# Two layers of attention and routed feed-forward on one core: the first tile of the output projection is placed and ordered anew, and the steps between projection, routing and the next layer are spread differently

## The chip, the cores and the metric

The kernel runs on one core of one Trainium2 chip. The metric is the device time of that core in microseconds. The kernel before took 4644.64 us (median of three runs, 4642.4 to 4648.78). Engines are named as in the profile: PE is TensorE (PEld its weight loads), DVE VectorE, ACT ScalarE, POOL GpSimd, SP SyncE. SP, ACT and POOL also issue DMAs, each from a queue of its own that works in order; a "q" behind the name (SPq, ACTq) marks the engine's sequencer.

## What is computed

Two layers, each of softmax attention and of a feed-forward block for the 8 tokens with the highest router score; both layers use the same weights.

```python
def _A_ref(x, wqkv, wo):          # x: 1 x 2048 x 1024, 32 heads of 32
    q, k, v = ...                 # from x @ wqkv
    p = softmax(q k^T * Dh ** -0.5)
    return (p v) @ wo
def _B_ref(x, w_r, w_gate, w_up, w_down):
    r = x @ w_r                   # router score of each token
    idx = argsort(-r)[:8]
    y = (silu(x_sel @ w_gate) * (x_sel @ w_up)) @ w_down     # F = 3584
    y = y * sigmoid(r_sel)
    return x + scatter_add(0, idx, y)
for _ in range(2):
    x = x + _A_ref(layernorm(x), wqkv, wo)
    x = x + _B_ref(layernorm(x), w_r, w_gate, w_up, w_down)
```

## The kernel before

**Order of work.** The program order is written out by hand: each engine runs its instructions in the order in which the Python code issues them, and waits only on data and on buffers. A buffer of a pool is handed on when all users of its last tile are done. Every product in high precision is made of three: a float32 matrix is split into a rounded high part and the rest, the low part, and high x high, low x high and high x low are summed in PSUM. ACT makes the high part with a cast, DVE or POOL the low part with a subtraction.

**A layer** (`layer`, called with n = 0 and n = 1) has three stages.

1. *Projection of q, k, v.* 96 steps `k`, each 24 products of 128x512 (a pass). Four blocks `c` of 512 tokens; in the first block of the second layer, steps 8, 12, 16 and 20 also take the statistics of a further tile and normalise it (`ln_stat`, `ln_norm`, L707 to 712), and every even step splits the next weight block (`split_w`, L686: one ACT cast, one POOL subtraction of 128x2048) and loads another (`load_w`). `ln_stats` (L138) ends in two small POOL operations that give `rs`, for which `ln_norm` on DVE waits. `proj` (L764) ends with an ACT cast `hi` and a DVE subtraction `lo`.
2. *Attention.* 32 units (head group x query chunk) of 16 key tiles; for each tile scores, exponential into `P` (nine buffers), products with v, and a running sum `ACC` of the exponentials over the key tiles. For the last unit DVE alone adds tiles 1 to 13 to tile 0, and `sum_mm` (L972) lets PE sum over the keys: first the tiles in `DIRECT` (14, 15), then `ACC`. Sums go to DRAM, come back by halves (`sum_load`, a tile of 64x512), are inverted on DVE (`recip`, L1001) and go out again.
3. *Output projection*, 16 token tiles `t` (L1141 to 1202). Of a tile: `load_o` (output `ord` and inverted sums, from DRAM: one and four DMAs, two buffers), `scale_o` (DVE), `split_o` (ACT cast `ohl`, DVE subtraction), 48 products of 128x512 against the weights' high parts `woh` and low parts `wol`, in three runs over the eight weight rows (L1148), then on DVE the residual sum (L1168), statistics (L1177), `xn` (L1188) and the router score (L1192), which overwrites the PSUM tile. PSUM has two such tiles (`ps_pre`), so tile t+2 starts after tile t's L1192. `load_o(t + 4)` is issued on ACT. Before tile 0, ACT casts eight weight rows (L1122) and DVE and POOL make their low parts (L1129). The second half of the sums (`second`) lies in the place of `xn`, so that `xn` of tile 0 waits until it is written out.

**Where things lie.** Pools are stacked. In the first layer the pool `wf` (`ord`, `ohl`, `woh`) stands behind the next layer's projection pool, since that layer's generator `nxt` is started first (L1067 to 1074); `ord` of tile 0 then falls into `KS[1]`, the keys, which the last scores read. In the second layer `ord` is the first of `wf` and falls into `KS[1]` too. The three query buffers `q0`, `q1`, `q2` are used in turn by the units.

**What the layers share.** Layer 1 is a generator that runs a piece at each `next(nxt)` inside the last tiles of layer 0's output projection: load weights and four tiles, statistics and normalisation of tiles 0 to 3, split of the first weights, transposes (`ln_tr`, L714: PE, ACT high part, DVE low part L739). The feed-forward block of layer 0 is worked off inside layer 1's projection: `stage` is the routing, in pieces that end at `yield`; `first_stage` runs beside the tiles after `CT` = 9, `second_stage` in steps 3 to 9 of layer 1's projection, one piece a step. `stage` ends with a gather and a scatter of rows on POOL's queue (L314, L315), and the scatter waits for the gather's data. `second_stage` ends with L346 to L350 on DVE and PE. Then `tick` works off four feed-forward steps and `refill` loads their weights (at steps 10, 14, ... and 11, 15, ...), and `permutation` (L352, at steps 13 and 17) has POOL write three tiles of 8x8 (`vb`) for PE.

## Time and profile before

| what | value |
|---|---|
| median of three runs | 4644.64 us |
| the profiled execution | 4644.15 us |
| its span, first to last instruction | 4642.1 us |
| busy share: PE, DVE, ACT, POOL | 97%, 69%, 52%, 69% |
| mean granted PE clock | 0.988 |
| first projection, attention, output projection of layer 0 | about 0 to 570, 570 to 2036, 2036 to 2235 us |
| the same of layer 1 | about 2235 to 2885, 2885 to 4347, 4347 to 4537 us |
| last feed-forward block | about 4537 to 4642 us |

The profile is of one execution. A row of the timeline has the start in us from the span's start, the duration, the engine, the line of the code, the operation, what is written and read, the count of instructions that are merged in the row, and in brackets the engine's idle time before it with what ended that. A row of the waits has the waiting instruction, what it waited for, the sum of the waits in us, their number and the longest. A row of the windows has the busy time of each engine in a stretch with its instruction count, then the granted PE clock, the busy share of the DMA engines and GB/s.

### The profile page before, as it was taken

To read this page: it belongs to the slowest core of one execution; us is meant where nothing else is said; L and a number is where in the kernel's file an instruction comes from. 1 tells how busy PE (TensorE), PEld (TensorE's weight loads), DVE (VectorE), ACT (ScalarE), POOL (GpSimd) and SP (SyncE) were. 2 spreads that over 40 slices of the span, in tenths; PEclk is the share of its full clock that TensorE was granted. 3 is DMA by queue.
4 is the path that set the end of the run, shared out by engine and by line. 5 is a ranking of instruction groups with operands and counts; after the bars stand their busy time and mean duration, and the time that the engine had idled before them with its cause. 6 is when DMAs were issued, how large, how long until landed. Compare 5 with 4: busy or idle time off the path is not lost. (4 is left out here: it accounts for less than half of the span.)

```text
span 4642.1 us, 73520 instructions
## 1 busy us (share of the span) xinstructions
PE 4520.6 (97%) x29224; PEld 2688.0 (58%) x29224; DVE 3183.7 (69%) x4945; ACT 2428.9 (52%) x2568; POOL 3219.2 (69%) x1247
## 2 busy tenths in 40 slices
PE   9999999999999999989899999999999999999896
PEld 7888755555555555448667786555555555554572
DVE  2211588888888888876422215888888888887763
ACT  3322267676767667750122222776676767677400
POOL 4444288988989898844433342988888899898441
PEclk9999999999999999999899999999999999999997
DMA  6757477776877777658489774777777768676597
GB/s 202 207 175 209 131 162 168 156 174 143 179 153 158 171 153 169 158 139 230 133 289 291 236 216 129 164 158 165 160 161 160 171 147 180 150 169 159 150 250 310
DMA packets 329301, 833.50 MB, mean 180 GB/s; under 512 B 44118, under 2 KB 159830, under 8 KB 279790
## 3 DMA queue, kind: packets, MB, share of 16 engines
q1 hardware_dynamic: 275214, 476.95, 35.0%
q0 software_dynamic: 45216, 325.57, 34.6%
q10 hardware_dynamic: 8528, 26.29, 2.2%
q8 instruction: 229, 3.75, 0.3%
q14 instruction: 114, 0.93, 0.1%
HBM read 384.24 MB, written 119.37 MB: 108 GB/s over the span
## 5 line engine op out<-in xcount | busy, mean ns | idle before, releaser
L639 DVE TENSOR_REDUCE nm<-st 128x1 f32<-128x512 f32 x3916 | 2433.7, 683 | 374.0 <-PE st L631 368.2
L1031 ACT ACTIVATE P<-pre 128x1024 f32<-128x1024 f32 x2048 | 1986.2, 1022 | 720.8 <-PE pre L646 522.2
L967 POOL TENSOR_TENSOR acc<-acc,P 128x2048 f32<-128x2048 f32 x434 | 2103.8, 4848 | 80.4 <-DMA P<-P 72.5
L646 PE MATMUL pre<-q,ks 64*128 64x512 f32 (+1 forms) x8192 | 1142.7, 396 | 4.3 <-ACT P L1031 4.3
L957 PE MATMUL pv<-P,v 128*32 128x512 f32 x8192 | 1091.9, 605 | 5.1 <-DMA v<-vd 5.1
L631 PEld LDWEIGHTS st<-ks,q 64*128 64x128 f32 x3916 | 546.5, 184 | 906.6 <-DVE nm L639 764.7
L631 PE MATMUL st<-ks,q 64*128 64x512 f32 x3916 | 980.6, 469 | 0.4
L646 PEld LDWEIGHTS pre<-q,ks 64*128 64x128 f32 (+1 forms) x8192 | 770.8, 186 | 190.7 <-ACT P L1031 57.4
L970 POOL DMA_DIRECT2D P<-P x310 | 296.4, 956 | 264.1 <-PE st L631 193.0
L775 DVE TENSOR_TENSOR lo<-st,hi 128x512 fp32r<-128x512 f32 x128 | 88.5, 691 | 568.4 <-ACT hi L774 562.7
L697 POOL TENSOR_TENSOR ohl<-wraw,ord 128x2048 fp32r<-128x2048 f32 x48 | 220.6, 4597 | 338.0 <-ACT ord L694 329.4
L697 POOL TENSOR_TENSOR wl<-wraw,wh 128x2048 fp32r<-128x2048 f32 (+1 forms) x49 | 221.1, 4512 | 303.8 <-ACT wh L694 285.0
L774 ACT CAST hi<-st 128x512 fp32r<-128x512 f32 x128 | 75.4, 589 | 564.1 <-PE st L760 564.1
L957 PEld LDWEIGHTS pv<-P,v 128*32 128x32 f32 x8192 | 161.8, 108 | 261.6 <-issue 253.3
L967 POOL TENSOR_TENSOR acc<-P 128x2048 f32<-128x2048 f32 x62 | 294.7, 4753 | 9.1 <-ACT P L1031 9.1
L1157 PE MATMUL pre<-woh,ohl 128*128 128x512 f32 x1024 | 245.3, 398 | 25.9 <-DVE pre L1192 14.4
L1157 PEld LDWEIGHTS pre<-woh,ohl 128*128 128x128 f32 x1024 | 195.9, 192 | 72.5 <-issue 17.2
L760 PE MATMUL st<-xh,wh 128*128 128x512 f32 x512 | 201.2, 393 | 0.0
L760 PE MATMUL st<-xh,wl 128*128 128x512 f32 x512 | 199.5, 390 | 0.0
L760 PE MATMUL st<-xl,wh 128*128 128x512 f32 x512 | 199.3, 389 | 0.0
L1101 ACT CAST ohl<-ord 128x1024 fp32r<-128x1024 f32 x32 | 33.6, 1051 | 309.6 <-DVE ord L1093 184.7
L760 PE MATMUL st<-woh,ord 128*128 128x512 f32 x512 | 166.8, 401 | 0.0
(344 smaller groups left out, 3866.7 us busy)
## 6 DMA issues: line engine op xcount, KB each, us to landing
P<-P POOLq DMA_DIRECT2D x310, 1024.0 KB, 8.8
wraw<-in_A_wqkv_dram SPq DMA_DIRECT2D x96, 1024.0 KB
q<-qh SPq DMA_DIRECT2D x256, 128.0 KB
ks<-kh SPq DMA_DIRECT2D x112, 256.0 KB
vd<-vn SPq DMA_DIRECT2D x32, 512.0 KB
qh<-hi SPq DMA_DIRECT2D x64, 256.0 KB
ql<-lo SPq DMA_DIRECT2D x64, 256.0 KB
kh<-hi SPq DMA_DIRECT2D x64, 256.0 KB
```

The costliest lines, as they stand in the source:

```text
L631: pe.matmul(ps[b], Q[u][rows, i, 0, qt * 128:(qt + 1) * 128], KS[(u // QC) % 2][rows, i, 0, j * 512:(j + 1) * 512], start=True, stop=True, ...
L639: dve.tensor_reduce(NM[u][:, j, 2 * i + b:2 * i + b + 1, qt], ps[b], axis=AX.X, op=OP.max, negate=True)
L646: pe.matmul(p[:, b * 512:(b + 1) * 512], KS[(u // QC) % 2][rows, i, slot, kt * 128:(kt + 1) * 128], Q[u][rows, i, slot, :], start=(slot == ...
L697: pool.tensor_tensor(wl[:, sl], raw[:, sl], wh[:, sl].bitcast(F32), op=OP.subtract)
L760: pe.matmul(p, *pair(a, l, r), start=(a == 0 and k == 0), stop=(a == KD - 1 and k == 2))
L774: act.copy(hi, p)
L775: dve.tensor_tensor(lo, p, hi.bitcast(F32), op=OP.subtract)
L957: pe.matmul(PV[u][32 * h:32 * h + 32, :], V[g][:, kt, 32 * h:32 * h + 32], P[s][:, h, :], start=(kt == 0), stop=(kt == NT - 1), tile_posit ...
L967: (dve if on_dve else pool).tensor_tensor(o, a, P[u * NT + k].rearrange("p h c -> p (h c)"), op=OP.add)
L970: pool.dma_start(P[u * NT + a], P[u * NT + b], accum_op=OP.add)
L1031: act.activation(P[s][:, 2 * i:2 * i + 2, :].rearrange("p h c -> p (h c)"), p, AF.Exp, scale=SCALE)
L1157: pe.matmul(p[:, bl], l[:, a, :], r[a][:, bl], start=(k == 0 and a == 0), stop=(k == 2 and a == KD - 1))
```

## The change

The last unit's tile 13 is summed by PE and no longer by DVE. The half sums are tiles of 128x256 and no longer of 64x512. In layer 0 the pool `wf` is opened ahead of `nxt`, so that `ord` takes the place of `q0`; in layer 1 `woh` is taken first from `wf`, so that `ord` falls into a buffer of v. Before tile 0, the casts, copies and subtractions are issued in another order, all low parts of weights on DVE; tile 0's first two runs of products go weight row by weight row. In each tile the low part is issued after the statistics (the closure `low`). The routing's pieces and the pieces of layer 1 come at other points of the tiles, and the statistics of two tiles go ahead of their normalisations. `stage` has one more `yield`, between the gather and the scatter. `vb` is written by DVE. Ticks and refills come one step later. The first two weight blocks of layer 1 get their low parts in four pieces. Some small tiles have three buffers, for which `pad` gives up room.

```diff
+LAST_DIRECT = (13, 14, 15)
...
-    cons.tile([128, 48], F32, name="pad")
+    cons.tile([128, 16], F32, name="pad")
...
-        st = small.tile([128, 2, 6], F32, name="bst")
+        st = small.tile([128, 2, 6], F32, name="bst", bufs=3)
...
             self.gather(tg, abi[:, 0:1], dst)
-            self.scatter(abi[:, 1:2], tg, dst)
...
+            yield
+            self.scatter(abi[:, 1:2], tg, dst)
...
-                pool.tensor_scalar(vb, ones_c[:, 0:8], PERM[i]["v"][:, j:j + 1], None, op0=OP.mult)
+                dve.tensor_scalar(vb, ones_c[:, 0:8], PERM[i]["v"][:, j:j + 1], None, op0=OP.mult)
...
                 ln_stat(0)
+                ln_stat(1)
+                yield
                 ln_norm(0)
-                yield
-                first_w = split_w()
+                ln_norm(1)
+                first_w = split_w(4)
                 next(first_w)
                 yield
-                ln_stat(1)
-                ln_norm(1)
-                yield
+                ln_stat(2)
+                ln_stat(3)
                 list(first_w)
                 load_w(blocks[2][1])
                 yield
-                ln_stat(2)
-                ln_stat(3)
                 ln_norm(2)
                 ln_norm(3)
...
-                    list(split_w())
+                    list(split_w(4 if n else 1))
...
-                    if k % 4 == 2 and k >= 10:
+                    if k % 4 == 3 and k >= 11:
                         for _ in range(4):
                             prev.tick()
-                    if k % 4 == 3:
+                    if k % 4 == 0:
                         prev.refill()
...
-                parts = [P[u * NT + k] for k in DIRECT] + [ACC.pop(u).rearrange("p (h c) -> p h c", h=4)]
+                parts = [P[u * NT + k] for k in (DIRECT if u < NU - 1 else LAST_DIRECT)] + [ACC.pop(u).rearrange("p (h c) -> p h c", h=4)]
...
-                return a[i * 8:i * 8 + 8].rearrange("t h (a g) c -> (t h a) (g c)", a=2)
+                return a[i * 8:i * 8 + 8].rearrange("t h (a g) c -> (t h a) (g c)", a=4)
...
-        if nxt:
-            next(nxt)
...
         wf = wfs.enter_context(sbuf(f"wf{n}", bufs=2))
+        if nxt:
+            next(nxt)
...
                 act.copy(oh, raw)
-                dve.tensor_tensor(ol, raw, oh.bitcast(F32), op=OP.subtract)
+
+                def low():
+                    dve.tensor_tensor(ol, raw, oh.bitcast(F32), op=OP.subtract)
+                return low
...
+            if n:
+                woh = weights(wf, "woh")
             load_o(0, sync)
             OT[0] = halves_o()
-            woh = weights(wf, "woh")
+            if not n:
+                woh = weights(wf, "woh")
...
             scale_o(0)
+            store_o(NU - 1, rest[:, 0:512])
             for a in range(KD):
                 act.copy(woh[a], WOR[:, a, :])
                 if a == 0:
-                    store_o(NU - 1, rest[:, 0:512])
-                if a == 3:
+                    low = split_o(0)
+                if a == 1:
+                    low()
                     store_sum(NU - 1, last_sum, rest[:, 512:1024])
-                    split_o(0)
-                eng = pool if a in (4, 6) else dve
-                eng.tensor_tensor(wol[a], WOR[:, a, :], woh[a].bitcast(F32), op=OP.subtract)
-            split_o(1)
-            second = XN[0:64, 0:512]
+                if a >= 1:
+                    dve.tensor_tensor(wol[a - 1], WOR[:, a - 1, :], woh[a - 1].bitcast(F32), op=OP.subtract)
+                if a == 5:
+                    scale_o(1)
+                    OT[1] = halves_o()
+            low = split_o(1)
+            dve.tensor_tensor(wol[KD - 1], WOR[:, KD - 1, :], woh[KD - 1].bitcast(F32), op=OP.subtract)
+            low()
+            second = XN[:, 0:256]
...
+                products = [(k, l, r, a) for k, (l, r) in enumerate(((oh, woh), (ol, woh), (oh, wol))) for a in range(KD)]
+                if t == 0:
+                    products.sort(key=lambda e: (e[0] == 2, e[3]))
...
-                        if first_stage and t > CT and k == 2 and a in (0, 6):
+                        if first_stage and k == 2 and (t - CT, a) in ((0, 7), (1, 0), (1, 6), (2, 0), (2, 6), (3, 0)):
                             next(first_stage, None)
-                        if nxt and t >= NT - 3 and (k, a) == (2, 0):
-                            next(nxt)
...
-                if nxt and t in (NT - 4, NT - 1):
+                if nxt and t == NT - 1:
                     next(nxt)
...
-                if t + 2 < NT:
-                    split_o(t + 2)
+                low = split_o(t + 2) if t + 2 < NT else None
...
-                if nxt and t >= NT - 2:
+                if nxt and t == NT - 1:
                     next(nxt)
                 mv, rs = ln_stats(x2)
+                if low:
+                    low()
+                if first_stage and t == CT + 3:
+                    list(first_stage)
+                    next(nxt)
+                if nxt and NT - 3 <= t < NT - 1:
+                    next(nxt)
...
+                if nxt and NT - 3 <= t < NT - 1:
+                    next(nxt)
...
-                if nxt and t in (CT, NT - 3):
+                if nxt and t == CT:
                     next(nxt)
```

More of the change, by code (lines that the diff above doesn't have):

```diff
@@ L51, in unit_events @@
     if last:
-        return [(k + 1, "mid", 1, "add", (k, 0 if k == 1 else None, True)) for k in range(1, NT) if k not in DIRECT]
+        return [(k + 1, "mid", 1, "add", (k, 0 if k == 1 else None, True)) for k in range(1, NT) if k not in LAST_DIRECT]
     ev = [(at, "end", 0, "merge", (k, k + 1)) for at, k in MERGED]
@@ L138, in ln_stats @@
     def ln_stats(xt):
-        st = small.tile([128, 2, 6], F32, name="bst")
+        st = small.tile([128, 2, 6], F32, name="bst", bufs=3)
         for i in range(2):
             dve.bn_stats(st[:, i, :], xt[:, i * 512:(i + 1) * 512])
-        mv = small.tile([128, 2], F32, name="mv")
+        mv = small.tile([128, 2], F32, name="mv", bufs=3)
         dve.bn_aggr(mv, st)
-        rs = small.tile([128, 1], F32, name="rs")
+        rs = small.tile([128, 1], F32, name="rs", bufs=3)
         pool.tensor_tensor(rs, mv[:, 1:2], eps_c, op=OP.add)
@@ L310, in stage @@
             dve.tensor_tensor(ab[:, 1:2], ab[:, 1:2], tcol, op=OP.add)
-            abi = perm["ab"] = cons.tile([8, 2], I32, name=f"ab{i}")
+            abi = cons.tile([8, 2], I32, name=f"ab{i}")
             dve.tensor_copy(abi, ab)
@@ L691, in split_w @@
                 W[wb] = [w.rearrange("p (a c) -> p a c", a=KD if wb < 8 else 4) for w in (wh, wl)]
-                for i in range(parts):
-                    sl = slice(2048 // parts * i, 2048 // parts * (i + 1))
+                sls = [slice(2048 // parts * i, 2048 // parts * (i + 1)) for i in range(parts)]
+                for sl in [slice(0, 2048)] if n else []:
                     act.copy(wh[:, sl], raw[:, sl])
-                    if n:
-                        yield
+                    yield
+                for sl in sls:
+                    if not n:
+                        act.copy(wh[:, sl], raw[:, sl])
                     pool.tensor_tensor(wl[:, sl], raw[:, sl], wh[:, sl].bitcast(F32), op=OP.subtract)
@@ L923, in layer @@
             assert not pairs
+        if prev:
+            prev.wf_end.close()
         wor = None
@@ L1045, in layer @@
                 if s == NS - 20:
-                    first = aw.tile([128, 512], F32, name="sm", bufs=1)[0:64]
+                    first = aw.tile([128, 512], F32, name="sm", bufs=1)[:, 0:256]
                     sum_load(first, 0)
@@ L1109, in layer @@
             ffn.tmp, ffn.wf, ffn.wf_end = wp, wf, wfs
+            if n:
+                woh = weights(wf, "woh")
             load_o(0, sync)
             OT[0] = halves_o()
-            woh = weights(wf, "woh")
+            if not n:
+                woh = weights(wf, "woh")
             wol = weights(wp, "wol")
@@ L1147, in layer @@
                     first_stage = ffn.first_stage(rcols)
-                for k, (l, r) in enumerate(((oh, woh), (ol, woh), (oh, wol))):
-                    for a in range(KD):
+                products = [(k, l, r, a) for k, (l, r) in enumerate(((oh, woh), (ol, woh), (oh, wol))) for a in range(KD)]
+                if t == 0:
+                    products.sort(key=lambda e: (e[0] == 2, e[3]))
+                if True:
+                    for k, l, r, a in products:
                         if part and k == 2 and a in (2, 6):
                             next(part)
-                        if first_stage and t > CT and k == 2 and a in (0, 6):
+                        if first_stage and k == 2 and (t - CT, a) in ((0, 7), (1, 0), (1, 6), (2, 0), (2, 6), (3, 0)):
                             next(first_stage, None)
-                        if nxt and t >= NT - 3 and (k, a) == (2, 0):
-                            next(nxt)
                         for bl in halves:
```

4 lines of the change are left out of this document (2 added, 2 removed).

## The prediction, made before the changed kernel ran

> **What bounds the kernel now.** I read the page's busy shares, then the waits of PE, then the timeline at each long wait. PE is the bound nearly everywhere: the span less PE's busy time leaves 121.5 us, so reordering can bring no more than that, and what the slow clock behind a long wait costs.
>
> ```profile
> span 4642.1 us, 73520 instructions
> PE 4520.6 (97%) x29224; PEld 2688.0 (58%) x29224; DVE 3183.7 (69%) x4945; ACT 2428.9 (52%) x2568; POOL 3219.2 (69%) x1247
> ...
> PE pre L1157 <- DVE pre L1192: 14.4, 7, 3.8
> PE st L358 <- POOL vb L357: 9.9, 4, 4.6
> PE st L235 <- DVE fy L232: 1.6, 1, 1.6
> ```
>
> My sum is the stalls that go, less those that stay or come. Work on PE keeps its length, and all that follows a place moves up with it.
>
> **Start of the output projection, layer 0: 7.3 us.**
>
> ```profile
> 1997.99 37.01 DVE L967 TENSOR_TENSOR acc<-acc,P 128x2048 f32<-128x2048 f32 x12
> 2029.49 0.34 SPq L1080 DMA_DIRECT2D ord<-oT  x1
> 2032.23 1.05 ACT L1122 CAST woh<-wor 128x1024 fp32r<-128x1024 f32 x1 [1.31 <-PE pv L957]
> 2035.05 1.07 PE L977 MATMUL st<-acc,ones 128*32 128x512 f32 x8 [1.17 <-DVE acc L967]
> 2037.38 1.23 DVE L1093 TENSOR_TENSOR ord<-ord 128x1024 f32<-128x1024 f32 x1 [2.39 <-DMA ord<-rd]
> 2039.74 5.42 PE L1157 MATMUL pre<-woh,ohl 128*128 128x512 f32 x16 [3.62 <-ACT ohl L1101]
> 2040.71 5.73 POOL L1129 TENSOR_TENSOR wol<-wor,woh 128x1024 fp32r<-128x1024 f32 x2 [31.83 <-ACT woh L1122]
> 2044.14 3.38 DVE L1102 TENSOR_TENSOR ohl<-ord,ohl 128x1024 fp32r<-128x1024 f32 x1
> 2047.58 3.92 PE L1157 MATMUL pre<-woh,ohl 128*128 128x512 f32 x16 [2.42 <-DVE ohl L1102]
> 2054.96 7.42 PE L1157 MATMUL pre<-woh,ohl 128*128 128x512 f32 x32
> ```
>
> Between attention and tile 1 (2054.96) PE stands three times: for the running sum, for `ord`, whose load SP could issue only when the scores had left its place (2029.49) and which lands at 2037.38, and for the low part of `ord`, which waited behind weights. The 16 products after the 3.62 us wait take 5.42 us, those after the 2.42 us wait 3.92: the slow clock behind a long wait costs 1.5. The 32 products at 2054.96 take 7.42 us; about 0.16 of it is the last one's tail, so one costs 0.227, a run of 16 3.63, a tile 10.9.
>
> After: without tile 13 DVE ends its sums 37.01 / 12 = 3.1 us sooner, at 31.9. `ord` has been there for long, since `q0` falls free when unit 30 ends, about 16 key tiles before the last scores; so `scale_o` ends at 33.2. ACT sets the pace: from 32.23 (the products with v are done) a copy of half a cast's width, nine casts of 1.05, and the copy of the sums come to 10.6 us, with gaps 10.9: the eighth weight row at 43.1. PE sums tile 13 in the time in which it waited, starts tile 0 near 35.9 and follows ACT's casts; behind the last cast stand four products (0.9) and the third run (3.6): tile 1 at 47.7 in place of 54.96. DVE's chain is shorter: low part of `ord`, eight weights and a `scale_o` at about 1.2 each from 35.1 end at 47, as the third run needs its last row at 47.2. POOL's two weights move to DVE, and this costs nothing as long as DVE's rows come to 1.2; beside POOL the low part took 3.38. If they take 1.9, tile 0 waits 6 us at its end; bounds 2 to 8.
>
> **The second half of the sums, tile 2: 5.3 us.**
>
> ```profile
> 2059.86 3.34 DVE L1002 RECIPROCAL xn<-xn 64x512 f32<-64x512 f32 x1
> 2067.52 0.81 DVE L1188 TENSOR_SCALAR xn<-x,mv,rs 128x1024 f32<-128x1024 f32 x1 [2.95 <-DMA rd<-xn]
> 2069.81 1.69 PE L1157 MATMUL pre<-woh,ohl 128*128 128x512 f32 x4 [3.81 <-DVE pre L1192]
> ```
>
> Tile 2 waits for tile 0's L1192, and this for the store of the inverted sums. 128 partitions of 256 halve the inversion (by the element, 1.7 us), and the low part goes behind the statistics. Tile 0's residual sum starts at 48.1, `scale_o` ends at 50.5, the inversion at 52.2; the store (here from the inversion's end at 63.2 to 67.5, 4.3 us) ends at 56.5, L1188 and L1192 at 58.7, when PE asks for the tile: 58.6. The wait of 3.81 and the slow clock go. Bounds: 0 if the store stays queued behind loads, 5.5.
>
> **Routing beside tiles 9 to 12: 1.6 us.** The wait L235 on L232 goes, since its two pieces come to lie most of a tile apart; the other pieces keep 2.7 us, in which DVE has to do under 2.
>
> **Border of the layers: 11.5 us.**
>
> ```profile
> 2205.44 0.89 POOL L213 DMA_INDIRECT x<-fw,ab  x1 [6.34 <-DMA fw<-x,ab]
> 2209.53 1.50 PE L1157 MATMUL pre<-woh,ohl 128*128 128x512 f32 x4 [2.56 <-DVE pre L1192]
> 2223.97 2.31 PE L1157 MATMUL pre<-woh,ohl 128*128 128x512 f32 x9 [1.70 <-DVE pre L1192]
> 2226.90 4.60 POOL L697 TENSOR_TENSOR ohl<-wraw,ord 128x2048 fp32r<-128x2048 f32 x1
> 2226.97 5.08 DVE L712 TENSOR_SCALAR xt<-xt,mv,rs 128x1024 f32<-128x1024 f32 x1 [1.76 <-POOL rs L146]
> 2243.63 1.12 PE L731 MATMUL st<-ident,xt 128*128 128x128 f32 x4 [7.20 <-DVE woh L739]
> 2244.39 0.78 PE L760 MATMUL pre<-ord,woh 128*128 128x512 f32 x1
> ```
>
> The scatter held POOL for 6.34 us ahead of `rs`, so L1192 came late and tile 14 waited 2.56; tile 15 waited 1.70; then the transposes stood 7.20 us, since DVE still had statistics and norms of the next layer's tiles ahead of their low parts. From tile 13's end (2209.53 - 2.56 = 2206.97) to the first product of layer 1 are 37.4 us. After, the scatter comes behind `rs`, and all four norms are issued before tile 15 ends: two tiles (21.8), 16 transposes (about 0.14 each from the row at 2243.63: four in 0.6, hence 2.3). Without stalls that is a gain of 13.3. Against it: L712 took 5.08 beside POOL's 4.60 where 0.81 is its own time (as L1188's above). The norms of tiles 0 and 1 will meet POOL's residual sum, those of tiles 2 and 3 the four quarters of the weight's low part, 4.60 / 4 = 1.15 each. I take 1.8 us off, between 0 and 4.60: 11.5.
>
> The Trainium skill, "SBUF — State Buffer", section "Who interferes with whom", says that VectorE and GpSimd share one port pair as an exclusive lock, held for a whole instruction. The row at 2226.97 agrees (it ends 0.55 us after POOL's). By it whole, all of POOL's 4.60 could stand ahead of the norms; the term would be 8.7 and the sum 44.7.
>
> The scatter now holds up POOL's output rows and, through them, SP's loads of the next tiles; those have a tile of time.
>
> **Routing in layer 1: 9.4 us.**
>
> ```profile
> 2302.36 0.89 POOL L213 DMA_INDIRECT x<-fw,ab  x1 [5.99 <-DMA fw<-x,ab]
> 2303.28 4.50 POOL L697 TENSOR_TENSOR ohl<-wraw,ord 128x2048 fp32r<-128x2048 f32 x1
> 2308.60 0.81 DVE L712 TENSOR_SCALAR xt<-xt,mv,rs 128x1024 f32<-128x1024 f32 x1 [11.65 <-POOL rs L146]
> 2310.18 0.80 DVE L346 TENSOR_SCALAR fw<-bg,mg 8x1024 f32<-8x1024 f32 x1
> 2311.03 1.02 PE L349 MATMUL st<-ident,fw 8*128 8x8 f32 x8 [11.14 <-DVE fw L346]
> ```
>
> The scatter's wait, the weight's low part, `rs`, the norm, `lo`, L346: a line through POOL and DVE in which PE's transposes stand last. After, the scatter is issued a pass later, so the low part runs in the gather's time, and the transposes come a pass (24 x 0.227 = 5.45) later. What stays: PE ends a pass, then ACT's `hi` (about 0.6), DVE's `lo` (about 0.7), two small ones and L346 (0.80): 2.4 us. The slow clock set in behind 2.56 us (the row at 2209.53, four products in 1.50) and not behind 2.42; I take half of 1.5. 11.14 + 1.5 - 2.4 - 0.75 = 9.5, less a little: 9.4, bounds 8.6 and 10.2.
>
> The Trainium skill, "TensorE: Matmul & The Clock Gate", section "Why this matters for your kernels", lets the clock fall only behind gaps of over about 3 us. The wait of 2.56 us does not fit that; by the rule this term would be 10.2 and the sum 48.3.
>
> **Permutation, steps 13 and 17: 0.4 us.**
>
> ```profile
> 2337.33 1.91 ACT L694 CAST ord<-wraw 128x2048 fp32r<-128x2048 f32 x1 [1.52 <-DMA wraw<-in_A_wqkv_dram]
> 2344.60 1.30 POOL L357 TENSOR_SCALAR vb<-ones,v 8x8 f32<-8x8 f32 x3
> 2344.97 0.20 PE L358 MATMUL st<-ident,vb 8*8 8x8 f32 x2 [4.34 <-POOL vb L357]
> 2345.39 0.67 DVE L775 TENSOR_TENSOR lo<-st,hi 128x512 fp32r<-128x512 f32 x1
> ```
>
> `vb` on POOL waits behind the weight's low part and `rs`. On DVE it waits behind the norm, which waits for the same `rs`, and behind `lo`, until 2346.1: later by 1.4 us, less about 0.3 for faster small operations. But with ticks a step later the projection's weight is asked for ahead of three feed-forward loads and not behind them, the 1.52 us of the cast go, and the chain moves up by them. So 0.2 at each; bounds -2.4 (no earlier weight) and 1.
>
> **Layer 1's output projection: 12.0 us.**
>
> ```profile
> 4349.96 5.53 PE L1157 MATMUL pre<-woh,ohl 128*128 128x512 f32 x16 [3.12 <-ACT ohl L1101]
> 4357.79 3.92 PE L1157 MATMUL pre<-woh,ohl 128*128 128x512 f32 x16 [2.30 <-DVE ohl L1102]
> 4379.01 2.32 PE L1157 MATMUL pre<-woh,ohl 128*128 128x512 f32 x9 [2.79 <-DVE pre L1192]
> 4400.00:4450.00 50.00, 48.83 (x216) 40.14 (x215) 32.17 (x38) 4.21 (x4) 22.18 (x29) 1.00 1.03 271
> 4429.03 9.65 ACTq L1082 DMA_DIRECT2D ord<-rd  x4
> ```
>
> The start has 0.6 less to lose than layer 0's: 6.7. Tile 2's 2.79 goes as above: 2.8. Of the 14.4 us of waits for L1192, 14.4 - 3.81 - 2.56 - 1.70 - 2.79 = 3.5 are left, in three tiles of this layer. There the DMA engines are full (share 1.03), and the four issues for `ord` hold ACT's queue for 9.65 us; the cast behind them is late, and the low part, statistics, `rs`, `xn`, L1192 follow. With the low part behind the statistics L1192 ends some 2.5 us sooner after it. PE runs further ahead of the loads, too; I take 2.5 of 3.5, bounds 0 and 3.5.
>
> **Sum.** 7.3 + 5.3 + 1.6 + 11.5 + 9.4 + 0.4 + 12.0 = 47.5. The profiled execution took 4644.15 us, 2.0 more than its span, for work around it, and 0.5 less than the median of the runs: 4644.15 - 47.5 = 4596.7, against the median 4597.
>
> **Rivals.**
>
> *Loads pace layer 1's output projection.* At 271 GB/s and a full share, PE's earlier start would buy waits for `ord`; the last 12.0 go: 4609. For it: the window above. The Trainium skill, "DMA: Bandwidth & Descriptors", section "Issuing engines are not separate DMA queues", has all queues on the same engines, which is this rival. Against it: every load there hangs on a tile's end and moves up with it.
>
> *POOL and DVE block each other at the two routing places.* The norms wait for all of the low part, and half of 11.5 + 9.4 is given back: 4607.
>
> *The permutation's stalls vanish* (4.34 and slow clock, twice): 4586. It needs `lo` and the norm to be ahead of time; the rows above speak against it.
>
> *`ord` does not come early*, for another user of that place: 7.3 + 6.7 go, 4611.
>
> *Slower: late weights in layer 1's first projection.* Ticks in the odd steps put a refill right ahead of every second weight load.
>
> ```profile
> 2400.00:2450.00 50.00, 50.00 (x249) 37.47 (x248) 12.09 (x19) 12.81 (x13) 19.85 (x8) 1.00 0.96 313
> ```
>
> The DMA engines are at 0.96 and 313 GB/s. Were the weight a pass late in each of the 12 rounds, 12 x 5.45 = 65 us were lost: 4662. It decides from 47.5 / 12 = 4 us a round. Against it: PE is fully busy in that window, and a split is issued two passes before its use.
>
> **How the numbers follow.** The forecast 0.55 (its own range 4589 to 4605), loads 0.15, POOL and DVE 0.13, permutation 0.06, `ord` 0.04, late weights 0.07. I stretch the range from 4586, the permutation's case, to 4618, beyond the three cases at 4607 to 4611 and up to some of their mixtures. A difference under 0.2% (9.3 us) can't be told from none. Faster: all but late weights, less 0.03 for mixtures that end within 9 us: 0.90; the same 0.03; slower 0.07.
>
> **What would show it.** Right: tile 0 runs without a wait over 1 us and lasts about 12; no wait of PE for L1192 over 1 us in tiles 2, 14 and 15; first product of layer 1 about 26 us after tile 13; L349 waits 2 to 3 us; L358 still 4 to 5, now for DVE. Wrong: L712 or L739 with rows over 3 us at the border, PE waiting for `ohl` of later tiles or for the split weights, or `ord` landing after 2032.

## The result, and the profile after

The changed kernel takes 4589.07 us (median of four runs, 4586.65 to 4590.93); the kernel before, run beside it on the same chip, 4645.48 us. The ratio is 0.9878, with an interval of 0.9861 to 0.9895. The forecast of 4597 us was 8 us too high; the time lies inside the stretched range of 4586 to 4618, near its lower end, and it meets the forecast's own range (4589 to 4605) by only 0.07 us. Run again with three of the experiments, the changed kernel took 4590.67 us (4587.88 to 4592.4) at a ratio of 0.9872 [0.9857, 0.9887].

The head of the page of the changed kernel, and below it three rows of its PE waits (waiting instruction, what it waited for, sum in us, number, longest):

```profile
span 4584.6 us, 73549 instructions
PE 4510.2 (98%) x29240; PEld 2684.3 (59%) x29240; DVE 3155.5 (69%) x4953; ACT 2428.1 (53%) x2568; POOL 3229.8 (70%) x1243
```

```profile
PE st L361 <- DVE vb L360: 8.5, 4, 4.1
...
PE st L352 <- DVE fw L349: 2.4, 1, 2.4
...
PE st L736 <- DVE woh L744: 0.5, 1, 0.5
```

PE stands 74.4 us in place of 121.5 (span less busy), and its busy time is 10.4 us shorter, although it has 16 more matmuls: for the most part, I take it, that is work that ran at the slow clock behind long waits and no longer does (the mean granted clock rises from 0.988 to 0.992). Of the five groups of waits that the sum was built on, those for `ohl` at the two starts (6.7 us for the high part and 4.7 for the low part before) have no row any more, and neither has the router score's in tiles 2 to 15 (14.4 us before, L1192; now L1218); the transposes' 7.2 has become 0.5, the 11.1 for the routed rows (`xg` in the code, `fw` in the rows) is 2.4, and only the permutation's 9.9 is still there, as 8.5. The score's wait is not gone for good: in a second profile of the changed kernel PE waits for it three times, 3.3 us in all (0.80 at tile 2 of layer 0, 1.12 and 1.36 at tiles 9 and 12 of layer 1).

The next rows are the timeline of the changed kernel from the end of layer 0's attention to tile 3 (start, duration, engine, line, operation, written and read, count, idle time before):

```profile
2032.42 1.22 DVE L1098 TENSOR_TENSOR ord<-ord 128x1024 f32<-128x1024 f32 x1
...
2035.41 7.77 PE L1177 MATMUL pre<-woh,ohl 128*128 128x512 f32 x32
2035.89 5.76 DVE L1142 TENSOR_TENSOR wol<-wor,woh 128x1024 fp32r<-128x1024 f32 x5
...
2046.82 7.45 PE L1177 MATMUL pre<-woh,ohl 128*128 128x512 f32 x32
...
2051.49 0.34 SPq L79 DMA_DIRECT2D rd<-xn  x1
...
2055.16 0.81 DVE L1214 TENSOR_SCALAR xn<-x,mv,rs 128x1024 f32<-128x1024 f32 x1 [1.43 <-DMA rd<-xn]
2056.00 1.23 DVE L1218 SCALAR_TENSOR_TENSOR pre<-xn,wrb 128x1024 f32<-128x1024 f32 x1
...
2057.74 7.42 PE L1177 MATMUL pre<-woh,ohl 128*128 128x512 f32 x32
```

`scale_o` (L1098) starts without a wait, since `ord` is there; tile 0 starts at 2035.41 with no idle time before it and lasts 11.4 us; tile 1 starts at 2046.82, where it started at 2054.96. The score L1218 ends before tile 1 does, so tile 2 follows at once. The store of the inverted sums still holds L1214 for 1.43 us, which hides behind tile 1.

The border of the layers and the two places in layer 1's first projection, on the same timeline:

```profile
2201.78 1.70 DVE L717 TENSOR_SCALAR xt<-xt,mv,rs 128x1024 f32<-128x1024 f32 x2
...
2210.89 2.51 DVE L717 TENSOR_SCALAR xt<-xt,mv,rs 128x1024 f32<-128x1024 f32 x2
2211.34 5.69 POOL L702 TENSOR_TENSOR ohl<-wraw,ord 128x512 fp32r<-128x512 f32 x4
...
2215.70 0.66 PE L736 MATMUL st<-ident,xt 128*128 128x128 f32 x4 [0.53 <-DVE woh L744]
...
2216.11 0.48 PE L765 MATMUL pre<-ord,woh 128*128 128x512 f32 x1
...
2277.87 0.67 PE L352 MATMUL st<-ident,fw 8*128 8x8 f32 x8 [2.37 <-DVE fw L349]
...
2305.39 0.33 PE L361 MATMUL st<-ident,vb 8*8 8x8 f32 x4 [4.06 <-DVE vb L360]
```

Layer 1's first product starts at 2216.11 (before: 2244.39). To see where the time came from I compare when PE starts the same product in the two profiled executions; the difference is the lead of the changed kernel, and what it grows by between two places is what was won there.

| between | won, us | forecast |
|---|---|---|
| program start to layer 0's last scores | 0.1 | 0 |
| to L0 tile 1 | 8.0 | 7.3 |
| L0 tile 1 to tile 3 | 5.65 | 5.3 |
| L0 tile 3 to tile 13 | 1.1 | 1.6 |
| L0 tile 13 to the second pass of layer 1 | 15.0 | 11.5 |
| to pass 11 (routing) | 9.5 | 9.4 |
| to pass 20 (permutation) | 2.0 | 0.4 |
| to layer 1's last scores | -0.45 | 0 |
| to L1 tile 1 | 7.5 | 6.7 |
| L1 tile 1 to tile 3 | 3.05 | 2.8 |
| L1 tile 3 to tile 15 | 4.35 | 2.5 |
| to the end | 1.7 | 0 |
| all | 57.4 | 47.5 |

### The profile page after: what moved, and what is told of

Same layout as the page of the kernel before. It is cut to its first block, busy times and chain, and to the rows that moved or that the text cites. A ratio compares the mean times of both kernels' runs of the same rounds, so it can differ in the third digit from the quotient of the medians.

```text
span 4584.6 us, 73549 instructions
## 1 busy us (share of the span) xinstructions
PE 4510.2 (98%) x29240; PEld 2684.3 (59%) x29240; DVE 3155.5 (69%) x4953; ACT 2428.1 (53%) x2568; POOL 3229.8 (70%) x1243
## 4 chain that ended last, share of the span: by engine, by line
PE 94%; DMA 2%; POOL 1%; issue 1%; DVE 1%; ACT 0%; SPq 0%; POOLq 0%; ACTq 0%; DVEq 0%
PE pv L962 22%; PE pre L649 21%; PE st L765 17%; PE st L634 16%; PE pre L1177 7%; PE pre L765 6%; PE st L982 4%; POOL acc L972 1%; PE pv L492 1%; PE pre L634 1%; PE pv L765 0%; PE pre L736 0%; POOL ohl L702 0%; PE st L521 0%; DMA v<-vd 0%
## 5 line engine op out<-in xcount | busy, mean ns | idle before, releaser
L702 POOL TENSOR_TENSOR ohl<-wraw,ord 128x2048 fp32r<-128x2048 f32 (+1 forms) x54 | 222.1, 4118 | 337.8 <-ACT ord L697 329.2
L1177 PE MATMUL pre<-woh,ohl 128*128 128x512 f32 x1024 | 238.2, 390 | 0.0
L1177 PEld LDWEIGHTS pre<-woh,ohl 128*128 128x128 f32 x1024 | 191.9, 188 | 42.3 <-ACT ohl L1106 1.7
L146 POOL TENSOR_TENSOR rs<-mv,eps_c 128x1 f32<-128x1 f32 x64 | 30.1, 470 | 230.6 <-DVE mv L144 230.6
```

The source lines that it names most:

```text
L702: pool.tensor_tensor(wl[:, sl], raw[:, sl], wh[:, sl].bitcast(F32), op=OP.subtract)
L1177: pe.matmul(p[:, bl], l[:, a, :], r[a][:, bl], start=(k == 0 and a == 0), stop=(k == 2 and a == KD - 1))
```

## The experiments

Each is the changed kernel with one part undone, or with one thing more done. I compare the starts of the same products as in the table. Where nothing differs, two traces keep their distance to within 0.05 us over hundreds of products, so that single microseconds show. At a few places, though, profiles differ by 1 to 3 us where the code is the same: at tile 2 of layer 0, at the routed rows, at tiles 8 to 12 of layer 1 and in the last block. A loss of that size there can be chance. The medians tell less: between chips and runs they spread by a few us, and the kernel before, beside these, had 4647.65, 4651.06 and 4648.39 us. "Lost" below is by the traces, against the changed kernel's first profile.

**The place of the first tile undone** (the pool opened behind `nxt` again, and closed where it was before, `ord` first of its pool in layer 1).

```diff
...
+        if nxt:
+            next(nxt)
...
         wf = wfs.enter_context(sbuf(f"wf{n}", bufs=2))
-        if nxt:
-            next(nxt)
...
-            if n:
-                woh = weights(wf, "woh")
             load_o(0, sync)
             OT[0] = halves_o()
-            if not n:
-                woh = weights(wf, "woh")
+            woh = weights(wf, "woh")
```

> The changed kernel with the first tile of the output projection in the place of before in both layers (the keys of the last group), all else as changed. Theory: the load is issued when the last scores are done, about 15 us later than in the changed kernel, and lands some 8 us after that; ACT's cast of the tile stands ahead of the other weights' casts, so all of them wait: 5 us a layer, 4599 in all (4595 to 4602). Rival: the earlier load alone buys little, since ACT's casts of the weights set the pace: under 2 us a layer.

4601.6 us (4597.01 to 4602.55), ratio 0.9894 [0.9878, 0.9911]. From its timeline at tile 0 (L1097 and L1173 are L1098 and L1177 of the changed kernel):

```profile
2037.45 1.23 DVE L1097 TENSOR_TENSOR ord<-ord 128x1024 f32<-128x1024 f32 x1 [4.30 <-DMA ord<-rd]
...
2039.81 0.80 PE L1173 MATMUL pre<-woh,ohl 128*128 128x512 f32 x1 [3.67 <-ACT ohl L1105]
```

The late load is back, at nearly the clock time of the kernel before (2037.38). Lost: 5.1 us by tile 1 in layer 0 and 5.2 in layer 1, of it 1.3 in layer 0 on the first products behind the wait, which run at the slow clock. A further 3.7 us go in tiles 8 to 12 of layer 1, on a wait of 1.83 us for the router score; the last section shows that this place differs between executions of one kernel.

**Tile 13 summed by DVE again** (`LAST_DIRECT = (14, 15)`).

> DVE sums tile 13 of the last unit again (one addition of 3.1 us more, four products of PE less). My theory: scale_o of tile 0 starts 3 us later, and with it the copy on ACT and DVE's whole chain, whose last low part of a weight ends now only 0.7 us before tile 0 does; so tile 1 starts 2 to 3 us later in each layer, with PE waiting for ohl or wol, 4 to 6 us in all. Rival: ACT's casts alone set the pace of tile 0 and DVE has 3 us to spare: no loss, and 0.9 us a layer less on PE.

4596.38 us (4594.92 to 4597.84), ratio 0.9886 [0.987, 0.9901]. The start of tile 0 on its timeline:

```profile
2034.73 1.22 DVE L1098 TENSOR_TENSOR ord<-ord 128x1024 f32<-128x1024 f32 x1
...
2037.07 9.30 PE L1177 MATMUL pre<-woh,ohl 128*128 128x512 f32 x32 [1.15 <-ACT ohl L1106]
```

DVE starts L1098 2.3 us later, ACT's cast of the tile with it, and tile 0 starts 1.7 us later, after a wait of PE of 1.15 us (and one of 1.20 for the running sum, 1 us of work earlier). The first seven products behind these waits run at the slow clock, their starts 0.29 to 0.67 us apart instead of 0.23, so the 32 take 9.30 us and not 7.77. Lost by tile 1: 3.1 and 2.4 us. The end of DVE's sums does set the start of tile 0; the rival, in which only ACT's casts count, falls.

**Tile 0's products in three runs again.**

```diff
-                if t == 0:
-                    products.sort(key=lambda e: (e[0] == 2, e[3]))
```

> The changed kernel with tile 0's products in three runs over the weight rows again. Theory: the first run is paced by ACT's casts to its end, and only then come the second and third run, 3.6 us each: tile 1 starts about 3.5 us later in each layer, 7 us in all (6 to 8): 4596. Rival: tile 0 is held by the low parts of the weights on DVE in any case; then under 1 us a layer.

4594.77 us (4592.36 to 4596.33), ratio 0.9881 [0.9864, 0.9897]. Two rows of its timeline:

```profile
2041.04 0.73 PE L1174 MATMUL pre<-woh,ohl 128*128 128x512 f32 x2 [0.22 <-ACT woh L1135]
2041.99 4.37 PE L1174 MATMUL pre<-woh,ohl 128*128 128x512 f32 x18 [0.21 <-ACT woh L1135]
```

Two products per weight row (0.45 us) are shorter than a cast (1.05), so PE stops for 0.2 to 0.5 us before each row, and the low part's products come behind all of them instead of filling the time. Lost: 2.9 and 2.8 us.

**Weight rows 4 and 6 on POOL again.**

```diff
-dve.tensor_tensor(wol[a - 1], ...)
+(pool if a - 1 in (4, 6) else dve).tensor_tensor(wol[a - 1], ...)
```

> The changed kernel with the low parts of weight rows 4 and 6 on POOL again. Theory: POOL's and DVE's two-input subtractions shut each other out, so DVE's rows take about 1.9 us in place of 1.2 and the last rows come late for the third run: 1 to 4 us a layer, 4591 to 4597. Rival: two engines share the work, DVE has two rows less to do and nothing waits: no difference, or 1 us less.

4594.13 us (4591.15 to 4597.78), ratio 0.9878 [0.9862, 0.9895]: the ratio sees no difference, the trace does. Its timeline beside tile 0:

```profile
2036.58 6.85 DVE L1142 TENSOR_TENSOR wol<-wor,woh 128x1024 fp32r<-128x1024 f32 x4
2039.78 5.90 POOL L1142 TENSOR_TENSOR wol<-wor,woh 128x1024 fp32r<-128x1024 f32 x2 [30.30 <-ACT woh L1135]
2043.36 3.41 DVE L1098 TENSOR_TENSOR ord<-ord 128x1024 f32<-128x1024 f32 x1
...
2047.96 2.61 PE L1177 MATMUL pre<-wol,ohl 128*128 128x512 f32 x6 [1.81 <-DVE wol L1142]
```

Beside POOL four rows take DVE 6.85 us, where five took 5.76 alone, and L1098 takes 3.41 where it took 1.22. What POOL takes over costs DVE more than doing it. Lost by tile 1: 2.8 and 2.1 us, and in layer 0 another 0.7 by tile 2, where products at the slow clock follow the wait of 1.81 us.

**The low part ahead of the statistics in every tile.**

```diff
-                low = split_o(t + 2) if t + 2 < NT else None
+                if t + 2 < NT:
+                    split_o(t + 2)()
...
-                if low:
-                    low()
```

> The changed kernel with each tile's low part issued at once again, ahead of the statistics. Theory: the low part waits for ACT's cast, so statistics, rs, xn and the router score come about 2.5 us later in every tile; this is hidden in layer 0, and in layer 1, where ACT's queue is held by its loads, PE waits for the router score's operation again: 2 to 4.5 us more in tiles 7 to 12, 4591 to 4594. Rival: those waits went because the loads came earlier against PE; then nothing changes there, and the time stays at 4589.

4612.53 us (4608.12 to 4624.15), ratio 0.9925 [0.9908, 0.9942]: some 23 us lost, far above what was expected. The row of its PE waits for the router score (L1217 here), and its timeline at tile 0's chain:

```profile
PE pre L1177 <- DVE pre L1217: 13.8, 6, 6.0
```

```profile
2050.61 1.23 DVE L1109 TENSOR_TENSOR ohl<-ord,ohl 128x1024 fp32r<-128x1024 f32 x1 [1.20 <-ACT ohl L1106]
2051.75 1.75 DVE L1007 RECIPROCAL xn<-xn 128x256 f32<-128x256 f32 x1
...
2053.52 0.34 SPq L79 DMA_DIRECT2D rd<-xn  x1
...
2058.96 0.81 DVE L1213 TENSOR_SCALAR xn<-x,mv,rs 128x1024 f32<-128x1024 f32 x1 [4.08 <-DMA rd<-xn]
...
2061.24 10.23 PE L1177 MATMUL pre<-woh,ohl 128*128 128x512 f32 x32 [3.56 <-DVE pre L1217]
```

DVE first stands 1.20 us for ACT's cast and then works 1.2 on the low part. The inversion starts 2.2 us later than in the changed kernel, its store ends later still (L1213 at 2058.96 in place of 2055.16), and tile 2 waits 3.56 us, nearly the 3.81 of before. So the halved inversion alone does not take this wait away; the order is needed. With the slow clock (32 products in 10.23 us, where the changed kernel takes 7.42) 6.5 us are lost by tile 3, more than the 5.65 that the whole change had won there. The same 2.4 us come back wherever the chain is tight: beside the routing (3.7 us), at tile 15 (1.6), and in layer 1 at tile 2 (a wait of 5.98) and in three later tiles (11.6 in that projection).

**The scatter next to the gather again** (the added `yield` in `stage` taken out).

> The changed kernel with the scatter issued right behind the gather (no yield between). Theory: in the second layer's projection POOL stands still for about 6 us at step 8 again, and PE's transposes of the routed rows wait 8 to 11 us at step 9 in place of 2.4 us at step 10: 7 to 10 us more, 4596 to 4599. At the border of the layers nothing over 1 us, since the gather was also moved to an earlier place in tile 12, so that rs of tile 12 is late by under 2 us. Rival: it was the scatter that delayed tiles 14 and 15; then these wait for L1192's operation again, and 4 us more are lost there.

4600.62 us (4600.12 to 4601.85), ratio 0.9896 [0.9879, 0.9912]. Its timeline at both places (L351 is L352):

```profile
2189.46 0.90 POOL L214 DMA_INDIRECT x<-fw,ab  x1 [6.90 <-DMA fw<-x,ab]
...
2274.33 0.88 POOL L214 DMA_INDIRECT x<-fw,ab  x1 [6.08 <-DMA fw<-x,ab]
2275.24 4.50 POOL L701 TENSOR_TENSOR ohl<-wraw,ord 128x2048 fp32r<-128x2048 f32 x1
...
2283.00 1.02 PE L351 MATMUL st<-ident,fw 8*128 8x8 f32 x8 [11.23 <-DVE fw L348]
```

At the routing the whole chain of before is back, with a wait of 11.23 us (before: 11.14), and 10.1 us are lost by pass 11. In layer 0 the scatter holds POOL for 6.90 us (6.34 before), but PE waits 1.12 at tile 14, not 2.56, and 1.3 us are lost there: more than the theory's nothing over 1, and less than the rival's 4. I take it that the other parts have made room there.

**The weight's low part at the border in one piece** (`split_w()` in place of `split_w(4)`).

> The changed kernel with the low parts of the second layer's first two weight blocks in one piece of 4.6 us each. Theory: POOL's long subtraction shuts out DVE's two-input and normalising operations while it runs, so the norms of tiles 2 and 3 (or the transposes' low parts) wait for up to 4.6 us, and from the end of tile 15 to the first product of the second layer it takes 2 to 4 us more than the 2.3 us of the changed kernel: 4591 to 4593. Rival: the pieces don't matter, since the norms come when POOL is done: no difference over 1 us.

4592.82 us (4590.85 to 4594.66), ratio 0.9879 [0.9862, 0.9895]. Its timeline at the border:

```profile
2210.96 5.79 DVE L717 TENSOR_SCALAR xt<-xt,mv,rs 128x1024 f32<-128x1024 f32 x2
2211.42 4.79 POOL L702 TENSOR_TENSOR ohl<-wraw,ord 128x2048 fp32r<-128x2048 f32 x1
...
2217.41 0.66 PE L736 MATMUL st<-ident,xt 128*128 128x128 f32 x4 [2.17 <-DVE woh L744]
```

The two norms take 5.79 us in place of 2.51, as POOL's 4.79 lie beside them. The wait of the transposes grows only from 0.53 to 2.17: 1.6 us for the quarters, less than the 2 to 4 expected.

**Ticks and refills at the steps of before.**

```diff
-                    if k % 4 == 3 and k >= 11:
+                    if k % 4 == 2 and k >= 10:
...
-                    if k % 4 == 0:
+                    if k % 4 == 3:
```

> The changed kernel with ticks and refills at the steps of before. Theory: the projection's weight is again asked for behind three feed-forward loads and lands late, so at steps 12 and 16 cast, low part, rs, norm come about 1.5 us later and PE's waits at steps 13 and 17 grow from 4.06 and 4.04 us to about 5.5 each; and the first tick follows the routed rows at once: 1 us more. 3 to 5 us in all, 4592 to 4594. Rival: the order of the loads doesn't matter; then the two waits stay at 4 us.

4593.63 us (4591.1 to 4597.3), ratio 0.9879 [0.9863, 0.9896]. From its timeline at the second permutation:

```profile
2333.15 1.91 ACT L697 CAST ord<-wraw 128x2048 fp32r<-128x2048 f32 x1 [1.16 <-DMA wraw<-in_A_wqkv_dram]
...
2342.08 0.33 PE L361 MATMUL st<-ident,vb 8*8 8x8 f32 x4 [5.28 <-DVE vb L360]
```

The cast waits 1.16 us for its weight again, and the permutation 5.28 us in place of 4.04: here the order of loads does move the chain. At the first permutation it does not: the cast does not wait, and PE's wait stays at 4.07, where 5.5 was expected. Lost from pass 11 to pass 20: 1.5 us.

**`vb` on POOL again.**

> The changed kernel with the permutation's three small tiles written by POOL again. Theory: the wait at steps 13 and 17 is set by the weight's low part and rs on POOL; on POOL the small tiles follow rs at once, on DVE they stand behind the norm and lo as well. So PE's waits at the two places (4.06 and 4.04 us, and 0.43 each for the third tile, in the changed kernel) become shorter by about 1 us each, and the time is the same or 2 us less (4587 to 4589). Rival: moving them to DVE was worth something; then the waits grow to 5 us or more, and the time by 2 us.

4588.4 us (4585.94 to 4592.31), ratio 0.987 [0.9854, 0.9887]. Its timeline at the second permutation, where the changed kernel waits 4.04 us:

```profile
2337.06 0.19 POOL L146 TENSOR_TENSOR rs<-mv,eps_c 128x1 f32<-128x1 f32 x1
...
2337.89 1.30 POOL L360 TENSOR_SCALAR vb<-ones,v 8x8 f32<-8x8 f32 x3
...
2338.25 0.20 PE L361 MATMUL st<-ident,vb 8*8 8x8 f32 x2 [2.78 <-POOL vb L360]
```

On POOL `vb` follows `rs` at once; on DVE it stands behind the norm (0.81) and `lo` (0.69). POOL's is the shorter wait, by 0.6 and 0.9 us at the two permutations once its later waits (0.32 at the first, 0.51 and 0.08 at the second) and those of the changed kernel (0.18 at each, not the 0.43 that I expected from) are counted. By the starts of the products only 0.5 us of it is won by pass 20, since more of them run at the slow clock behind. This part of the change costs a little; the medians do not show it.

**Both permutations at step 19, behind the ticks.** The wait that the change left is the largest in the projection.

```diff
-                    if k in (13, 17):
-                        prev.permutation(k // 17)
+                    if k == 19:
+                        for j in range(2):
+                            prev.permutation(j)
```

The changed kernel was run again beside this and the next:

> The changed kernel once more, unaltered, as the measure for the three others on the same chip. Its ratio to the kernel before should fall into the interval found already (0.9861 to 0.9895).

> Both permutations run at step 19 of layer 1's first projection, behind the ticks, and no longer at steps 13 and 17. My theory: the waits for vb (4.06 and 4.04 us, each with a second one of 0.43 and a stretch at the slow clock) come from POOL's low part of a weight and the norm that stand before vb on the chain in these two steps; in step 19 neither stands there, so the waits go: span 8 to 11 us shorter than the changed kernel's. Rival: the wait is vb's own way from DVE to PE at whatever place, so two waits of 2 to 4 us show at step 19 as well, and the span is within 3 us.

4578.55 us (five runs, 4576.48 to 4580.6), ratio to before 0.9847 [0.9834, 0.986]; all five lie below the four runs of the changed kernel on the same chip (4587.88 to 4592.4). Its timeline at step 19:

```profile
2343.45 0.33 PE L361 MATMUL st<-ident,vb 8*8 8x8 f32 x4 [0.20 <-DVE vb L360]
...
2344.55 0.33 PE L361 MATMUL st<-ident,vb 8*8 8x8 f32 x4 [0.40 <-DVE vb L360]
```

The two waits of 4 us are gone, and by pass 20 the trace has won 11.3 us: about 8 of waits, and 3 of products at the slow clock behind them (1.2 and 1.8 us in the changed kernel, by the distances of their starts). At the end of the trace 8.8 us of it are left, mostly because the last block takes 2.2 us longer, as it does in some profiles and not in others. The wait was the place in the chain, not `vb`'s way to PE.

**And PE's small transposes a step behind `xg`** (a `yield` more ahead of them).

> As the run before, and PE's eight small transposes come a step later than the xg that they read (one more yield ahead of them). My theory: the wait of 2.37 us at step 10 goes with the slow stretch behind it: 2 to 4 us less than the run before. Rival: the piece that now slides into the next step runs into the ticks or the next norm and gives a wait of its own, so that the two runs end within 1 us.

4578.16 us (4575.32 to 4579.36), ratio 0.9844 [0.9831, 0.9858]: as the run before. Its timeline shows why (L353 and L493 are L352 and L492):

```profile
2284.51 0.66 PE L353 MATMUL st<-ident,fw 8*128 8x8 f32 x8
...
2287.07 3.64 PE L493 MATMUL pv<-fw,xs 128*32 128x512 f32 x32 [1.90 <-DVE xs L354]
```

The 2.37 us wait is gone, but the first tick, in the same step now, waits 1.90 us for what the transposes deliver. At this place the trace wins 2.3 us more than in the run before, 1.6 of it a stretch at the slow clock that did not follow here; as the last section shows, such a stretch comes in one profile and not in the next, even behind the same wait. The medians do not show the gain. The rival's new wait is there, if somewhat smaller than the old one.

## Why the prediction was right, and what it mis-sized

**The start of the output projection** (7.3 and 6.7 forecast, 8.0 and 7.5 measured) went as argued: `ord` early, tile 0 from 2035.41 (35.9 forecast), tile 1 at 2046.82 (47.7). That ACT sets the pace held only just: tile 0's products start 0.23 us apart nearly throughout, and ACT's last cast of a weight ends at 2041.83, 0.3 us before the first product that needs it. Four experiments each take 2.1 to 5.2 us of the term away, in both layers, so no single part carries it. That POOL's two weights cost DVE nothing held (DVE's rows stayed at 1.15 to 1.2 apart); it even was the faster choice.

**The second half of the sums** (5.3, measured 5.65; 2.8 and 3.05 in layer 1): the size was right, but the prediction gave two causes side by side, the halved inversion and the low part behind the statistics. With the inversion halved and the low part in its old place the wait of tile 2 is back at 3.56 us. So it is shown that the inversion would not do alone; what it adds to the order was not tried. There is little to spare: in six of the twelve profiles that have the low part behind the statistics, tile 2 of layer 0 waits 0.6 to 1.0 us for the score again, and in the second profile of the changed kernel the term comes to 4.55.

**The border of the layers** (11.5, measured 15.0) is the term that was mis-sized most, by 3.5 us. The gain without stalls was put at 13.3 and came out at 13.4 by layer 1's first product; the 1.8 us taken off for VectorE and GpSimd blocking each other did not arise. The norms of the first pair took 1.70 for two, those of the second 2.51, and PE waited 0.53 us. The mechanism is real: with the low part whole, the norms took 5.79 us. But with the quarters they end almost in time. The other 1.55 us lie in the first pass: before, the 7.20 us wait was followed by products at the slow clock, which the sum had counted at other long waits and left out here. By the exclusive lock of the Trainium skill ("SBUF — State Buffer", section "Who interferes with whom"), held for a whole instruction, the prediction put the term at 8.7. The run with the low part whole shows norms that are held as the rule says, yet it loses only 1.6 us of the 15.0: the time ahead of the transposes covers the rest.

**Routing in layer 1** (9.4, measured 9.5): the chain of POOL's scatter, low part, `rs` and norm was read rightly; one `yield` undone brings all of it back. The wait of 2.4 forecast to stay is 2.37. In the second profile of the changed kernel, where no slow clock follows it, the term comes to 11.0.

**The permutation** (0.4, measured 2.0) was mis-sized, and its working slips: 1.52 less 1.1 gives 0.4 at each, not 0.2. Both opposite effects are there. `vb` on DVE costs about 0.7 us at each, less than the 1.1 forecast. Before, the cast waited for its weight at both places (1.52 and 1.75 us), in the changed kernel at neither. Ticks and refills account for 1.2 us of that, at the second place; what moved the first weight, and the second by the rest, no run shows. The waits fell from 9.9 to 8.5 us; of the other 0.6 us of the term, 0.2 is fewer products at the slow clock behind them, by the distances of their starts, and the rest stays open.

**Later tiles of layer 1** (2.5, measured 4.35) and the end (0, measured 1.7) hold what differs between executions. In the second profile of the changed kernel 3.2 of the 4.35 are not won, and 0.8 of the 1.7; over the profiles of the changed kernel and its variants the time from layer 1's tile 15 to the end runs from 115.5 to 118.4 us. The profiled run, at 4586.65, is itself 2.4 us below the median of its four, so that much of the 10 us beyond the sum is the draw of one execution. In the second profile 53.9 us are won, 6.4 beyond the sum. In neither profile does one big miss hide another: most terms came out at or above their forecast, and the total is too small for that reason.

**Beside tiles 9 to 12** 1.1 us were won of 1.6: the wait of L235 went, but one of 0.58 us at another piece (L251 on DVE's L247) came, which the sum had put at nothing.

**The rivals.** Late weights in layer 1's first projection, the slower case, did not come: between passes 20 and 95 the lead stays within 0.6 us. `ord` did come early. POOL and DVE blocking each other fell with the border's rows. The permutation's stalls did not vanish; that the time comes near this rival's 4586 is luck, since other terms brought it there. That loads pace layer 1's output projection fell as stated, since the 12 us came in full, but the weaker form of it is what makes the later tiles uncertain.

## What to carry to other kernels

An operation that nobody waits for at once belongs behind the ones that release the next tile, above all when it itself waits for another engine: moving one 1.2 us subtraction of each tile was worth some 20 us in the changed kernel, the largest of the parts tried. Where a small operation feeds PE at a fixed step, look for what its engine has queued ahead of it at that step, and move it to a step where nothing is; changing its engine only exchanges one queue for another. And price a long wait of PE with the products behind it that run at the slow clock, at each place.

## What the runs showed of the hardware

**The slow clock behind one and the same wait comes in one execution and not in the next.** The wait at `xg` is 2.37 us in ten profiles in which products of 128x512 follow it (the two of the changed kernel and eight of its variants). In seven of them six to eight products of 0.63 us came, at once or four products later, and in three none did; of the two profiles of the changed kernel one has them and one has not. The windows of 8 us around it, first of the changed kernel, then of the one with tile 0 in three runs (busy time of PE, PEld, DVE, ACT and POOL with counts, granted clock, DMA share, GB/s):

```profile
2276.00:2284.00 8.00, 6.13 (x25) 5.02 (x26) 1.85 (x5) 2.01 (x3) 4.56 (x1) 0.79 0.75 210
```

```profile
2279.00:2287.00 8.00, 6.09 (x32) 5.13 (x33) 1.85 (x5) 2.04 (x3) 4.60 (x1) 1.00 0.77 211
```

In the same busy time PE does 25 instructions at a granted clock of 0.79 and 32 at 1.00; 1.54 us hang on it between the two profiles of the changed kernel. The prediction's half of 1.5 was fair. The Trainium skill ("TensorE: Matmul & The Clock Gate", section "What's actually happening") says that the window in which activity is watched runs freely, which agrees with this. The Trainium skill's advice to leave no gaps above about 3 us ("TensorE: Matmul & The Clock Gate", section "Why this matters for your kernels") is too generous by these runs, where 2.37 us were enough in seven of ten profiles.

**Small DMA issues can hold an engine's compute for as long as a tile.** The four issues of `ord<-rd` on ACT's queue at one of layer 1's later tiles, in the first profile of the changed kernel and then in its second, there with DVE's wait for ACT's cast and PE's wait at tile 9:

```profile
4390.25 7.65 ACTq L1087 DMA_DIRECT2D ord<-rd  x4
```

```profile
4389.09 11.19 ACTq L1087 DMA_DIRECT2D ord<-rd  x4
...
4401.46 1.23 DVE L1109 TENSOR_TENSOR ohl<-ord,ohl 128x1024 fp32r<-128x1024 f32 x1 [4.74 <-ACT ohl L1106]
...
4404.89 7.54 PE L1177 MATMUL pre<-woh,ohl 128*128 128x512 f32 x32 [1.12 <-DVE pre L1218]
```

ACT's next cast comes only behind them (it starts 0.1 us after their end in both), then the low part and the score. At 7.65 us PE waits for nothing, at 11.19 for 1.12 us, and a wait of 1.36 follows three tiles later. The low part, now behind the statistics, still stands ahead of `xn` and the score on DVE, so these wait for the cast too; whether a place behind the score would spare PE the wait was not tried. The DMA engines are full in this stretch, as the window of the first profile shows (share 1.01):

```profile
4350.00:4400.00 50.00, 50.00 (x222) 41.42 (x221) 32.59 (x42) 5.25 (x5) 25.26 (x34) 1.00 1.01 290
```

Another way of loading the inverted sums was not tried either.
